# One written order of two thousand tokens in place of the priority scheduler, in an attention and MLP kernel on one core

## Chip, cores and metric

The kernel runs on one core of a Trainium2 chip. The metric is the device time of one execution in microseconds (us); less is better. The core's engines each work through their own queue in the order in which the program was laid out: TensorE (PE) multiplies, VectorE (DVE) and ScalarE (ACT) work elementwise, GpSimd (POOL) hardly takes part, and SyncE (SP) issues the DMAs. An instruction at the head of a queue that has to wait holds up all behind it.

## What is computed

Inputs of attention are q, k, v, a_re, a_im of shape (4, 8, 768, 48); the output of attention becomes 3072 tokens of 384, which go through an MLP with weights 384 x 2048 and 2048 x 384, all float32.

```
mag = np.sqrt(a_re * a_re + a_im * a_im)
scale = np.minimum(mag, 0.999) / (mag + 1e-06)
a_re_n, a_im_n = (a_re * scale, a_im * scale)
for t in range(S):                       # S = 768, per batch and head
    new_re = ar * S_re - ai * S_im       # ar, ai: a_re_n, a_im_n at t
    new_im = ar * S_im + ai * S_re
    S_re, S_im = (new_re + k[t] outer v[t], new_im)
    y[t] = q[t] @ S_re
h = x @ w_in                             # x: y as 3072 x 384
g = h - np.tanh(h)
out = g @ w_out
```

## The kernel before

The sequence is cut into six chunks of 128 positions. A *block* g (0 to 11) is one chunk of two batches: 256 tokens. A *unit* u (0 to 23) is one chunk of one batch; block g consists of the units 2g and 2g + 1. The names of the stages:

- *Gates* of a block: `gates_b` (magnitude: Ln and Exp on ACT), `gates_b2` (decay), `gates_c` (angle: Arctan, then running sums by matmuls with a triangle, line 220 or in f32 line 217), `gates_d` (cosine and sine) and `gates_e` (running sums, Exp into `g_e`, and the chunk's last row through a small DRAM buffer `hscr` into `hd`).
- `products` of a unit: q and k are multiplied by gates and waves on DVE, cast to an f16 pair (high part on ACT, remainder on DVE) and transposed, by DMA (`qT`, `kT`, line 408) or, for the first four units, which stay in f32, by TensorE. `vv` is the pair of v.
- `attention` of a unit (line 431): scores by matmul, masked on DVE into `af`, split into the pair `a`; the matmuls with the carried state `z` and with `vv` give y in PSUM; y is cast to f16 on ACT and its remainder taken on DVE (tile `x`), and one DMA transposes both into `xT`. Last comes the update of `z`.
- MLP of a block, in eight steps fp: `head` (line 510) is 18 matmuls of 256 columns into one of three PSUM buffers `h`, then tanh on ACT and h - tanh on DVE (tile `mt`); `split` makes the f16 pair `mg` of two steps; `tail` (line 540) is 12 matmuls of 384 columns into `o`. After step 7, o goes to the output by way of ACT and DMA.
- `decode`: 16 weight pairs come in as 64-bit words and are turned to f16 pairs, five operations on DVE and ACT each plus the remainder.

What sets the order: the text emits instructions by the lists START, FIRST, SECOND and CYCLE, which say after which head of a block which steps of other stages are issued, and each call carries a *kind* with an offset (OFFSET, for the first blocks EARLY), which the class `At` hands to `tc.high_priority`. The framework's priority scheduler then decides at build time the final order on each engine's queue and the buffers, from priorities and dependencies. Activations that need a table, and the table loads, are chained in the order of the text by `chained` (line 334). `tables` emits a load where the wanted set is not the current one. Most instructions are recorded at the wrapper's line 102, so groups are best told apart by their tiles.

Of the kernel before, what the change touches and what calls it, by code (L numbers as in the profile page):

```python
# [84 lines left out]

@with_exitstack
def tile_fast(ctx: ExitStack, tc: tile.TileContext, flag, a_in, qkv_in, win_in, wout_in, sq_c, vec_c, lim_c, out):
    nc = tc.nc
    V, G, A, T, SP = nc.vector, nc.gpsimd, nc.scalar, nc.tensor, nc.sync

    early = [True]

    class At:
        def __init__(self, eng, kind):
            self.eng, self.kind = eng, kind

        def __getattr__(self, n):
            f, offset = getattr(self.eng, n), (EARLY if early[0] else OFFSET)[self.kind]

            def call(*a, **k):  # L100
                with tc.high_priority(offset=offset):
                    return f(*a, **k)  # L102
# [23 lines left out]
    ps_a = ctx.enter_context(tc.tile_pool(name="ps_a", bufs=3, space=PSUM))  # L126

# [11 lines left out]
    araw = {}  # L139
    raws = {}  # L140

    def load_a(g):
        if g < NG:
            c, bp = divmod(g, 2)
            araw[g] = [sb.tile([P, 2 * HD], F32, name=f"a_raw{i}") for i in range(2)]
            for x in ((slice(0, HD), slice(HD, 2 * HD)) if g == 0 else (slice(0, 2 * HD),)):
                for t, i in zip(araw[g], range(2)):
                    SP("load").dma_start(out=t[:, x], in_=a_in[c * P:(c + 1) * P, bp, i, x])

    def load_qkv(u):  # L150
        if u < 2 * NG:
            c, b = divmod(u, B)
            raws[u] = sb.tile([P, 3, H, D], F32, name="qkv_raw", bufs=2)
            SP("load").dma_start(out=raws[u], in_=qkv_in[c * P:(c + 1) * P, b])

    load_a(0)
    vec = const.tile([P, 9], F32, name="vec")
    SP("load").dma_start(out=vec, in_=vec_c)
    sqc = const.tile([P, 4, P], F32, name="sqc")
# [98 lines left out]
    def gates_c(g, cols):  # L258
# [9 lines left out]
        for x in cols:  # L268
# [3 lines left out]
            if plain:  # L272
                continue
# [555 lines left out]
```

## Time and profile before

| what | us |
|---|---|
| three runs | 577.77, 577.37, 574.74 |
| median | 577.37 |
| profiled execution, span from first to last instruction | 570.2 |
| PE, DVE, ACT busy in it | 506.1, 452.8, 435.8 |
| first head of blocks 0, 1, 2, 3 begins | 69.8, 115.6, 158.0, 202.3 |
| first head of blocks 4 to 9 begins | 243.9, 285.4, 326.9, 368.4, 409.9, 451.1 |
| first head of blocks 10 and 11 begins | 489.4, 525.9 |
| last tail ends | 563.2 |

The profile gives the profiled execution's span and no device time beside it; the median of the runs is 7.2 us above that span. In the profile a group is written as line, engine, operation, out<-in; "idle before" is the time its engine stood still just ahead of its instructions and what ended most of that. PE's busy time is modelled at its ends. PEld are the weight loads, which run beside the matmuls. "L102" is the wrapper of `At`, so it tells nothing of the stage.

The first 70 us are spent on the gates, the weights and the f32 units of block 0, with TensorE mostly waiting. From there on blocks follow one another, every 41.5 us in the middle; while block g is projected, the attention of block g + 1 and the gates after it are worked in between. The last two blocks have less or no attention beside them.

### The profile page before, as it was taken

To read this page: it belongs to the slowest core of one execution; us is meant where nothing else is said; L and a number is where in the kernel's file an instruction comes from. 1 tells how busy PE (TensorE), PEld (TensorE's weight loads), DVE (VectorE), ACT (ScalarE), POOL (GpSimd) and SP (SyncE) were. 2 spreads that over 40 slices of the span, in tenths; PEclk is the share of its full clock that TensorE was granted. 3 is DMA by queue.
4 is the path that set the end of the run, shared out by engine and by line. 5 is a ranking of instruction groups with operands and counts; after the bars stand their busy time and mean duration, and the time that the engine had idled before them with its cause. 6 is when DMAs were issued, how large, how long until landed. Compare 5 with 4: busy or idle time off the path is not lost.

```text
span 570.2 us, 12229 instructions
## 1 busy us (share of the span) xinstructions
PE 506.1 (89%) x5058; PEld 389.4 (68%) x5058; DVE 452.8 (79%) x638; ACT 435.8 (76%) x784; POOL 2.3 (0%) x7
## 2 busy tenths in 40 slices
PE   2386399999999989989899899899899899999995
PEld 0164387876777767777677677687687677787772
DVE  4987999999898798798797897887986987953332
ACT  6978967998967967977968968959959959643442
POOL 1000000000000000000000000000000000000000
PEclk9976599999999999999999999999999999999998
DMA  7886822368184274286293383482672550730001
GB/s 253 244 313 179 256 63 51 76 135 188 24 199 130 49 165 133 44 142 160 57 190 100 79 168 99 101 165 81 126 150 71 130 144 15 130 90 15 29 1 33
DMA packets 133899, 68.08 MB, mean 119 GB/s; under 512 B 119982, under 2 KB 123694, under 8 KB 133836
## 3 DMA queue, kind: packets, MB, share of 16 engines
q1 hardware_dynamic: 133836, 67.23, 48.7%
q8 instruction: 41, 0.67, 0.5%
q14 instruction: 22, 0.18, 0.1%
HBM read 36.74 MB, written 4.78 MB: 73 GB/s over the span
## 4 chain that ended last, share of the span: by engine, by line
PE 44%; ACT 25%; DVE 16%; DMA 7%; issue 6%; SPq 1%; ACTq 0%; DVEq 0%
PE h L518 17%; PE o L549 15%; PE att L102 9%; DMA xT<-x 4%; ACT L102 4%; ACT a_raw L102 4%; ACT g_trig L102 3%; ACT mg L102 3%; ACT g_t L102 2%; DVE io L402 2%; DVE a_raw L102 2%; DVE qkv_raw L398 2%; DVE g_t L102 2%; PE att L217 2%; ACT mt L102 2%
## 5 line engine op out<-in xcount | busy, mean ns | idle before, releaser
L518 PE MATMUL h<-xT,w 128*128 128x256 f16 x1728 | 215.6, 274 | 23.1 <-DMA xT<-x 23.1
L549 PE MATMUL o<-w,mg 128*128 128x384 f16 x1152 | 206.1, 326 | 0.8 <-DVE mg L102 0.7
L518 PEld LDWEIGHTS <-w 128*128 128x128 f16 x1728 | 167.4, 98 | 54.6 <-DMA xT<-x 14.7
L549 PEld LDWEIGHTS <-mg 128*128 128x128 f16 x1152 | 110.6, 98 | 64.3 <-DVE mg L102 1.2
L102 DVE SCALAR_TENSOR_TENSOR mt<-h,mt 128x512 f32<-128x512 f32 x96 | 65.0, 686 | 40.0 <-ACT mt L102 39.5
L102 ACT ACTIVATE mt<-h 128x512 f32<-128x512 f32 x96 | 55.5, 590 | 43.4 <-PE h L518 43.2
L535 DVE SCALAR_TENSOR_TENSOR mg<-mt,mg 128x1024 f16<-128x1024 f32 x40 | 48.9, 1224 | 25.3 <-ACT mg L102 25.3
L102 ACT ACTIVATE mg<-mt 128x1024 f16<-128x1024 f32 x48 | 50.5, 1052 | 17.9 <-DVE mt L102 17.9
L102 ACT ACT_TABLE_LOAD x40 | 51.3, 1283 | 1.4 <-PEq L822 0.8
L102 PE MATMUL att<-qT,kT 96*128 96x128 f16 (+1 forms) x544 | 47.3, 235 | 1.1 <-ACT kT L102 0.7
L102 ACT ACTIVATE a_raw<-a_raw 128x768 f32<-128x768 f32 (+2 forms) x49 | 39.2, 802 | 1.7 <-DVE a_raw L102 1.7
L402 DVE TENSOR_TENSOR io<-qkv_raw,g_trig 128x768 f32<-128x768 f32 x40 | 36.9, 951 | 0.3
L119 DVE TENSOR_TENSOR qk<-io,qk 128x1536 f16<-128x1536 f32 x20 | 35.0, 1751 | 0.3 <-ACT qk L102 0.2
L102 DVE TENSOR_TENSOR a<-af,a 128x512 f16<-128x512 f32 x40 | 27.2, 684 | 8.5 <-ACT a L102 8.4
L102 ACT ACTIVATE a<-af 128x512 f16<-128x512 f32 x40 | 24.8, 626 | 11.8 <-DVE af L455 11.3
L102 PEld LDWEIGHTS <-kT 96*128 96x128 f16 x480 | 30.6, 97 | 3.2 <-DMA kT<-qk 0.8
L102 ACT ACTIVATE g_e<-att,vec 128x384 f32<-128x384 f32 x48 | 27.1, 572 | 4.4 <-PE att L217 4.3
L102 ACT ACTIVATE qk<-io 128x1536 f16<-128x1536 f32 x20 | 29.6, 1481 | 0.3 <-DVE io L402 0.3
L455 DVE TENSOR_TENSOR af<-att,sqc 128x512 f32<-128x512 f32 x36 | 24.5, 681 | 0.1
L102 DVE SCALAR_TENSOR_TENSOR g_t<-g_t,a_raw 128x768 f32<-128x768 f32 (+1 forms) x26 | 23.0, 889 | 0.7 <-ACT a_raw L102 0.7
L102 ACT ACTIVATE g_trig<-g_t 128x768 f32<-128x768 f32 (+1 forms) x26 | 20.3, 785 | 0.7 <-DVE g_t L102 0.6
L398 DVE SCALAR_TENSOR_TENSOR qkv_raw<-g_e,qkv_raw 128x768 f32<-128x768 f32 x20 | 19.0, 951 | 1.9 <-ACT g_e L102 1.9
(88 smaller groups left out, 602.4 us busy)
## 6 DMA issues: line engine op xcount, KB each, us to landing
qkv_raw<-in_qkv SPq DMA_DIRECT2D x24, 576.0 KB
a_raw<-in_a SPq DMA_DIRECT2D x22, 384.0 KB
io<-in_wout SPq DMA_DIRECT2D x16, 384.0 KB
io<-in_win SPq DMA_DIRECT2D x16, 384.0 KB
out_dram<-io SPq DMA_DIRECT2D x24, 192.0 KB
a_raw<-in_a SPq DMA_DIRECT2D x4, 192.0 KB
xT<-x SPq DMA_TRANSPOSE x24
hd<-hscr SPq DMA_DIRECT2D x20, 3.0 KB
```

The lines of the kernel that those rows point to most:

```text
L102: return f(*a, **k)
L119: by_name[ENGINE[which]](kind).tensor_tensor(**k)
L217: T("cum").matmul(c_ps[:, :HD], lhsT=tri32[which], rhs=hl[:, bb * HD:(bb + 1) * HD], start=True, stop=True)
L398: V("prod").scalar_tensor_tensor(out=x, in0=ee[:, :, sl], scalar=E_MAX, in1=x, op0=ALU.min, op1=ALU.mult)
L402: V("prod").tensor_tensor(out=f[:, i], in0=raw[:, i, :, None].broadcast_to([P, H, 2, D]), in1=tg[:, :, sl].rearrange("p r (h d) -> p h r d ...
L455: V("af").tensor_tensor(out=af.rearrange("p (j t) -> p j t", j=4), in0=s_ps.rearrange("p (j t) -> p j t", j=4), in1=(causal if plain else ...
L518: T("h").matmul(h_ps[:, j].rearrange("p (two t) -> p two t", two=2), lhsT=wi[ft][:, wp, kt * P:(kt + 1) * P], rhs=xT[:, :, xp, kt, :], sta ...
L535: V("glo").scalar_tensor_tensor(out=gg[:, 1], in0=th, scalar=2.0 ** SG, in1=gg[:, 0], op0=ALU.mult, op1=ALU.subtract)
L549: T("o").matmul(o_ps[:, tt, :DM], lhsT=gg[:, gp, fp % 2, j * 256 + tt * P:j * 256 + (tt + 1) * P], rhs=wo[ft][:, wp], start=(ft == 0 and n ...
```

## The change

All stages become generators ("streams"), named by a letter: T table load, c constants, A and Q loads, d decode (kind, pair), w, R and X statistics, B to E the gates of a block, p `products` of a unit, v its values, z the cast of the state, s scores (unit, half), y the matmuls to the transposed x, k the update of the state, h head, g split, o tail, O output. A stream yields after each instruction, or after each group of matmuls: h and o are yielded in two halves, 9 and 6 matmuls. `drive` walks through ORDER: each token advances its stream by one step, and `*n` by n steps; a T token always loads its table. The context `tc.manual_schedule()` makes the text's order the final one on all queues, and `At`, `copy`, `chained`, the lists and the offsets go. ORDER has 2,007 tokens, 2,089 steps. Tiles, buffer counts and the arithmetic stay; the constant 1.0 of the last check is set at the start. There are 52 T tokens. The diff, cut to its core (the passages of ORDER are from its start, the surroundings of block 0's first h, the passage around the start of block 6, and its end):

```diff
-LAG = 2
-START = (
-    "o3 i0 F0 F1 q0 i1 q1 p0 p1 B1 p0 i2 p1 o0 p0 b1 a0 p1 a1 a1 E1 C1 i7 a1 D1 a1 o6 a0 o4 i4 i5 o1 a0 o2 i3 B2 a0 "
-).split()
...
-CYCLE = tuple((int(i), x) for i, x in (y.split(":") for y in (
-    "0:p2 0:a1 3:p3 4:p2 4:p3 5:a2 5:a2 5:p3 5:a2 6:w0 6:a2 6:a2 6:a0 7:C2 7:a3 9:D2 10:B3 10:a3 10:E2 10:a3 11:a3 11:b3 11:p4 14:w1 "
-).split()))
...
+SETS = ("natural_log_exp_and_others", "trig_and_small", "sigmoid_and_others", "silu_and_others", "exp_and_others")
+ORDER = """
+A.0*2 T.0 B.0 A.0 c B.0*2 d.1.0 B.0 d.1.0 A.0 b.0*2 B.0 b.0*2 d.1.0 T.1 C.0 b.0 d.0.0 B.0 d.0.0 c E.0 b.0 d.1.1 d.1.0*2 C.0 d.1.0 Q.0 d.0.0 d.1.1 Q.1
+T.0 b.0 d.0.0 b.0 d.0.0 b.0 d.1.0 E.0 b.0 C.0 d.0.0 E.0 d.1.0 A.1 E.0 C.0 d.1.2 d.0.0 R.0 C.0 E.0 C.0 d.1.1 D.0 C.0 d.1.1 T.1 D.0 R.0 d.1.1 C.0 D.0*2
+d.1.2 v.1 R.1 C.0 D.0 p.0 A.1 d.0.0 D.0 d.1.1 d.0.3 p.0 T.0 E.0 p.0 p.1 R.1 p.0 B.1 p.0 p.1 d.0.3 p.0*2 B.1 p.1*3 d.0.4 v.0 p.1*2 d.1.2 d.0.2 p.0 p.1
+B.1 d.1.2 b.1 p.0*2 b.1 d.1.2 d.1.1 p.1 p.0*2 d.0.3 d.1.2 s.0.0 s.0.1 d.0.1 b.1 d.1.1 E.0 d.0.1 E.0 b.1 s.0.0 d.0.1 T.1 C.1 c b.1 p.1 Q.2 d.0.2 d.0.4
+p.1 d.0.1 C.1 d.0.3 C.1 s.0.1 d.0.1 d.0.5 d.0.3 d.0.1 C.1 d.1.2 d.0.5 C.1 d.0.3 d.0.1 C.1 d.0.3 d.1.2 C.1 d.0.1 p.1 Q.3 D.1 d.0.2 D.1 d.0.3 D.1 y.0
+d.0.2 d.0.6 d.0.5 R.2 y.0 d.0.4 d.0.5 s.1.0 d.0.2 s.1.1 d.0.5 d.0.4 C.1 A.2 s.1.0 v.2 y.0 A.2 d.0.4 y.0 d.0.2 y.0 T.0 B.2 E.1 B.2 s.1.1 d.0.4 y.1 B.2
...
+d.0.5*2 b.2 p.2*3 h.0.1 R.3 p.2 b.2 k.1 p.2 h.0.0 d.0.7 d.1.3 h.0.4 p.3 d.1.3 C.2 h.0.0 T.1 C.2 T.4 E.1 d.0.7 p.3 C.2 p.3 C.2 d.1.4 h.0.0 d.1.3 d.1.5
...
+k.12 s.13.1 E.6 o.4.7 O.4 y.12*2 B.8 O.4 s.13.1 k.13 O.4 p.14*2 v.15 h.5.5 g.5.1 s.13.0 o.5.0 h.5.6 h.5.4 b.8 s.13.1 b.8 O.4 p.15 y.12 p.14 b.8 o.5.0
+h.5.5 v.15 g.5.1 E.6 o.5.1 k.13 h.5.7 o.5.1 s.13.0 s.13.1 b.8 h.5.4 T.2 h.5.4 y.13 p.14 h.5.4 E.7 y.12 o.5.2 y.13 h.5.7 b.8 E.7 h.5.5 y.13 o.5.2 y.13
+y.12 s.14.1 v.14 h.5.7 h.5.5 b.8 s.14.0 v.14 y.13 g.5.2 b.8 s.14.1 o.5.3 C.8 h.6.0 E.8 y.13 p.15 C.8 o.5.3 g.5.2 C.8 T.4 E.8 C.8 Q.17 p.15 h.5.7 h.6.2
+s.14.0 h.6.0 o.5.4 C.8 h.6.3 p.15 o.5.4 h.6.2 z.14 s.14.0 E.8 Q.16 g.5.3 v.14 z.15 s.14.1 C.8 E.8 z.14 s.14.0 p.15 g.5.3 o.5.5 p.15 C.8*2 h.6.0*2 C.8
...
+h.11.7 o.11.3 g.11.2 o.11.4 g.11.2 o.11.4 h.11.7 o.11.5 g.11.3 o.11.5 g.11.3*2 R.23 o.11.6*2 o.11.7*2 X O.11 X*2 O.11*3
+"""
...
+def drive(streams, order):
+    live = {}
+    for token in order.split():
+        name, _, times = token.partition("*")
+        for _ in range(int(times or 1)):
+            if name not in live or name[0] == "T":
+                kind, *args = name.split(".")
+                live[name] = streams[kind](*map(int, args))
+            next(live[name], None)
+    for stream in live.values():
+        assert next(stream, "end") == "end"
+
...
-    early = [True]
-
-    class At:
-        def __init__(self, eng, kind):
-            self.eng, self.kind = eng, kind
-
-        def __getattr__(self, n):
-            f, offset = getattr(self.eng, n), (EARLY if early[0] else OFFSET)[self.kind]
-
-            def call(*a, **k):
-                with tc.high_priority(offset=offset):
-                    return f(*a, **k)
-            return call if offset else f
-
...
+    ctx.enter_context(tc.manual_schedule())
+
+    def cast(out, in_, scale=1.0):
+        A.activation(out=out, in_=in_, func=AF.Copy, scale=scale)
...
+    def tables(i):
+        table[0] = SETS[i]
+        A.preload_act_table_set(SETS[i])
+        yield
+
+    def act(func, **k):
+        assert table[0] in TABLES[func], (func, table)
+        A.activation(func=func, **k)
...
+    def mix(u):
+        g, bb = divmod(u, 2)
+        c = u // B
+        plain = u < PLAIN
+        qT = unit[u]["qT"]
+        y_ps = ps_a.tile([P, 512], F32, name="att")
+        if c > 0:
+            z16 = z16s[u]
+            for h in range(H):
...
+        cast(x16[:, 0], y_ps[:, :HD], ys)
+        yield
+        V.scalar_tensor_tensor(out=x16[:, 1], in0=y_ps[:, :HD], scalar=ys, in1=x16[:, 0], op0=ALU.mult, op1=ALU.subtract)
+        yield
+        if g not in xTs:
+            xTs[g] = sb.tile([P, 2, 2, KT, P], F16, name="xT", bufs=BUFS["xT"])
+        SP.dma_start_transpose(out=xTs[g][:, bb].rearrange("p two k t -> p (two k) t"), in_=x16.rearrange("p two e -> p (two e)"))
+        yield
+        A.activation(out=junk()[:, :HD // 8], in_=y_ps[:, :HD].rearrange("p (n s) -> p n s", s=8)[:, :, 0], func=AF.Square, scale=ys, accum_out=stat("x"))
...
+    drive({
+        "T": tables, "c": constants, "A": load_a, "Q": load_qkv, "d": decode, "w": weight_stats,
+        "B": ratio, "b": decay, "C": angles, "D": waves, "E": envelope,
+        "R": raw_stats, "p": keys, "v": values, "z": state, "s": scores, "y": mix, "k": update,
+        "h": head, "g": split, "o": tail, "O": emit, "X": check_stats,
+    }, ORDER)
```

More of the change, by code (lines that the diff above doesn't have):

```diff
@@ L137, in junk @@
         return sb.tile([P, 2, 512], F16, name="junk").rearrange("p a n -> p (a n)")
[L139 to L156, printed above, removed]
+    table = [None]
+    def tables(i):
[5 more added lines that the diff above has]
+        A.activation(func=func, **k)
     vec = const.tile([P, 9], F32, name="vec")
[L158 removed]
     sqc = const.tile([P, 4, P], F32, name="sqc")
[L160 removed]
     tri = const.tile([P, P], F16, name="tri")
[L162 removed]
     causal, mask, tri32, ident = sqc[:, 0], sqc[:, 1], (sqc[:, 0], sqc[:, 2]), sqc[:, 3]
@@ L277, in gates_c @@
+            if not plain:
+                ax = by_half(ai)
+                cast(hl[:, :, 0], ax, 1.0 / TWO_PI_F)
+                yield
+                V.scalar_tensor_tensor(out=hl[:, :, 1], in0=ax, scalar=1.0 / TWO_PI_F, in1=hl[:, :, 0], op0=ALU.mult, op1=ALU.subtract)
+                yield
         nf = sb.tile([P, W], F32, name="g_t1")
@@ new lines, in envelope, with raw_stats, keys @@
+                yield
+    unit = [{} for _ in range(2 * NG)]
+    def raw_stats(u):
+        sq = sb.tile([P, 3, D // 3], F32, name="rawsq")
+        A.activation(out=sq, in_=raws[u][:, :, u % H, :D // 3], func=AF.Square)
+        yield
+        V.tensor_reduce(out=stat("qkv", 3), in_=sq, axis=mybir.AxisListType.X, op=ALU.add)
+        yield
+    def keys(u):
+        g, bb = divmod(u, 2)
+        ee, raw = gate[g][0], raws[u]
+        sl = slice(bb * HD, (bb + 1) * HD)
+        wave = lambda: trig[g][:, :, sl].rearrange("p r (h d) -> p h r d", d=D)
+        if u < PLAIN:
@@ L412, in products, with values @@
+        yield
+        unit[u]["k"] = dst[:, 1]
+        for i in range(2):
+            dT = sb.tile([P, 2 * H, P], F16, name=("qT", "kT")[i], bufs=BUFS[("qT", "kT")[i]])
+            unit[u][("qT", "kT")[i]] = dT
+            SP.dma_start_transpose(out=dT, in_=dst[:, i].rearrange("p two h e -> p (two h e)"))
+            yield
+    def values(u):
+        v = raws[u][:, 2].rearrange("p h d -> p (h d)")
+        if u < PLAIN:
             vd = sb.tile([P, 512], F32, name="af", bufs=BUFS["af"])[:, :HD]
-            copy("vd", "vhi", vd, v, sVd)
@@ L465, in attention @@
-        a16 = [x[0] for x in a16]
-        y_ps = ps_a.tile([P, 512], F32, name="att")
-        if c > 0:
-            for h in range(H):
-                for n, (qp, zp) in enumerate(PASS):
-                    T("qu").matmul(y_ps[:, h * D:(h + 1) * D], lhsT=qT[0:K, qp * H + h], rhs=z16[0:K, zp, h * D:(h + 1) * D], start=(h == 0 and n == 0), stop=False)
-        yield "QU"
+        plain = u < PLAIN
+        kk, vv = unit[u]["k"], unit[u]["v"]
+        kv = ps_a.tile([P, 512], F32, name="att")
@@ L504, in attention @@
-        yield "Z"
+            for n, (kp, vp) in enumerate(PASS):
+                T.matmul(kv[:, h * D:(h + 1) * D], lhsT=kk[:, kp, h], rhs=vv[:, 2 + vp, h * D:(h + 1) * D], start=(h == 0 and n == 0), stop=(h == H - 1 and n == 2))
+        yield
+        z, src = z32[b][0:K], kv[0:K, :HD]
+        if c > 0:
+            V.scalar_tensor_tensor(out=z, in0=z, scalar=2.0 ** (SK + SV - SZ - STEP[-1]), in1=src, op0=ALU.mult, op1=ALU.add)
+            src = z
+            yield
+        hd = gate[g][1]
```

654 lines of the change are left out of this document (310 added, 344 removed).

## Prediction

> **What bounds the kernel now.** I read the page's busy line first, then the busy time of the engines in three stretches, then TensorE's waits.
>
> ```profile
> span 570.2 us, 12229 instructions
> PE 506.1 (89%) x5058; PEld 389.4 (68%) x5058; DVE 452.8 (79%) x638; ACT 435.8 (76%) x784; POOL 2.3 (0%) x7
> ```
>
> ```profile
> 0.00:69.80 69.80, 32.33 (x113) 23.79 (x114) 54.92 (x80) 56.03 (x99) 2.34 (x7) 0.79 0.79 248
> 69.80:158.00 88.20, 85.32 (x812) 67.61 (x812) 82.11 (x119) 78.34 (x136) 0.00 (x0) 0.98 0.40 92
> 158.00:570.20 412.20, 388.46 (x4136) 298.04 (x4133) 315.75 (x441) 301.43 (x551) 0.00 (x0) 0.99 0.46 103
> ```
>
> Columns of the second fence: stretch, length, then busy time of PE, PEld, DVE, ACT, POOL, granted clock, DMA share, GB/s. The stretches are cut at two first projections (h): block 0's starts at 69.76, block 2's at 158.01, and the rows of the timeline for these are
>
> ```profile
> 69.76 5.16 PE L518 MATMUL h<-xT,w 128*128 128x256 f16 x27 [9.19 <-DMA xT<-x]
> 158.01 2.13 PE L518 MATMUL h<-xT,w 128*128 128x256 f16 x18
> ```
>
> So there are three regimes. Until 69.8 TensorE has little to do and VectorE sets the pace (54.9 of 69.8). From there to 158.0 both are nearly full (PE 85.3, DVE 82.1 of 88.2), since the last weights are still decoded. From 158.0 on TensorE alone bounds: 388.5 of 412.2. Its idle time there is 23.7 us. Whom it waited for in that stretch, and the end of the chain of work that ended last:
>
> ```profile
> PE h L518 <- DMA xT<-x: 14.0, 7, 3.3
> PE att L220 <- ACT a_raw L102: 2.0, 8, 0.2
> PE o L549 <- DVE mg L102: 0.7, 1, 0.7
> ```
>
> ```profile
> 551.48 1.95 PE o L549 x12
> 553.43 1.97 PE h L518 x18
> 555.39 7.81 PE o L549 x48
> ```
>
> 14.0 us are seven waits for the transposed attention output xT at the head of a block, 2.7 are small waits, and 7.0 (570.2 - 563.2, where the last o ends) are the output's way home. 14.0 + 2.7 + 7.0 = 23.7, so the stretch is explained. In the two rows above it a full projection pair is 3.92 us without a gap, so PE's work itself is not compressible by an order. An order can only win in the 23.7 us and ahead of 158.0.
>
> The sums below are made against the span of the profiled execution, 570.2. The median of the three runs shown is 577.37, 7.2 more, and I add 7.2 to a span to get a time. A difference under 0.5% (2.9 us) is one that a measurement here can hardly tell from none.
>
> **Term 1, the start of block 2.** The new list puts 194 VectorE instructions ahead of block 2's first h; the old trace has 198 there (80 and 119 in the rows, one of them cut in two by the border). Sixteen weight pairs are decoded in both, and it is the same work but for four fewer on balance. What a short and a middling one cost:
>
> ```profile
> L102 DVE TENSOR_TENSOR a<-af,a 128x512 f16<-128x512 f32 x40 | 27.2, 684 | 8.5 <-ACT a L102 8.4
> L102 DVE TENSOR_SCALAR vv<-vv,vec 128x768 f16<-128x768 f16 x20 | 8.2, 411 | 0.0
> ```
>
> Four cost 1.6 to 2.7 us; I take 2.0 and get 54.9 + 82.1 - 2.0 = 135.0 us of VectorE work. The question is the idle time beside it: 14.9 us in the first stretch, 6.1 in the second. VectorE's waits in the first:
>
> ```profile
> DVE a_raw L102 <- ACT a_raw L102: 5.3, 2, 3.5
> DVE a L102 <- PE att L102: 2.6, 3, 1.0
> DVE x L102 <- ACT x L102: 2.0, 1, 2.0
> DVE w L102 <- ACT w L102: 1.3, 3, 0.9
> ```
>
> The first row is the very beginning (nothing is loaded yet), and the list begins the same way, so it stays. The other three the list fills: between the scores s.0.0 and the masking behind them stand two other VectorE instructions (the gate's lm, a decode's wlo), between y.0's cast and its remainder five (three of decodes, one mask, one value), and every wlo of a decode stands several places behind its whi. I count 2.6 + 2.0 + 1.3 = 5.9 us as gone, keep the rest: 9.0 + 6.1 = 15.1 idle. Start of block 2: 135.0 + 15.1 = 150.1. Bounds: 156.0 with the old 21.0 us of idle time, 144.0 if the 6.1 of the second stretch goes too. TensorE allows it: if block 0 begins 5.9 us earlier, at 63.9, and then needs 85.3 us less what is put off (next term), 82.4, plus its old 2.9 of idle time, it is there at 149.2.
>
> **Term 2, what is put off.** The list lets o trail h by more: ahead of block 2's first h it has 23 half tails of six matmuls, 138, where the old trace has
>
> ```profile
> L549 PE MATMUL o<-w,mg 128*128 128x384 f16 x156 | 28.3, 326 | 0.0
> ```
>
> by 158. Eighteen matmuls at 1.95/12 = 0.163 are 2.9 us that come later. The other TensorE work ahead of that point is the same.
>
> **Term 3, the block boundaries.** Old boundary, from the timeline (start, duration):
>
> ```profile
> 315.78 0.77 PE L477 MATMUL att<-vv,a 128*128 128x48 f16 x24
> 316.38 2.13 PE L518 MATMUL h<-xT,w 128*128 128x256 f16 x18
> 320.42 0.58 ACT L102 ACTIVATE x<-att,vec 128x384 f16<-128x384 f32 x1
> 321.50 0.61 DVE L102 SCALAR_TENSOR_TENSOR x<-att,vec,x 128x384 f16<-128x384 f32 x1
> 322.06 0.94 SPq L102 DMA_DIRECT2D hd<-hscr  x2
> 323.10 2.29 SPq L102 DMA_TRANSPOSE xT<-x  x1
> 326.91 1.26 PE L518 MATMUL h<-xT,w 128*128 128x256 f16 x10 [1.76 <-DMA xT<-x]
> ```
>
> The chain is: attention done (316.4), cast on ACT, remainder on DVE, transpose by DMA, first h at 326.9: 10.5 us, with 8.7 us of other matmuls as cover. 4.0 of the 10.5 the cast spent behind the gate's Exp calls on ACT; 1.0 the transpose spent behind the hd loads on SP's queue (x is done at 322.1, the issue is at 323.1). Without these two, 320.42 to 326.91 less 1.0 is 5.5 us.
>
> In the list I counted, for blocks 3 to 11, the matmuls between the second unit's y and the block's first h: half heads of 9 at 1.97/18, half tails of 6 at 1.95/12, gate sums as two matmuls of a tail's width, and the attention's small ones by
>
> ```profile
> 293.98 1.28 PE att L102 x36
> ```
>
> The cover is 6.7, 6.6, 8.7, 3.8, 10.4, 7.9, 4.7, 4.9, 6.9 us. ACT instructions between y and its cast: 0, 3, 2, 1, 8, 2, 1, 3, 0; DVE instructions between cast and remainder: 1, 3, 3, 0, 5, 0, 0, 0, 3. A block of the old trace gives their mean cost, 33.95/64 = 0.53 and 35.34/52 = 0.68:
>
> ```profile
> 285.40:326.90 41.50, 39.45 (x440) 30.47 (x440) 35.34 (x52) 33.95 (x64) 0.00 (x0) 1.00 0.54 119
> ```
>
> Chain less cover, where positive, with these queues in full: 2.5 (block 4), 2.2 (6), 2.7 (7), 1.3 (9), 2.2 (10), 0.6 (11): 11.5 us. With clear queues (5.5 everywhere): 1.7 + 0.8 + 0.6 = 3.1. With the old chain of 10.5 everywhere: 33.9. I take 8 for the old 14.0, nearer to the full queues, since two engines that are busy 82 and 85% of a block will mostly not have done those instructions before. On SP the list takes the hd loads away from just ahead of the transpose, but puts a transpose of k or the first unit's own there in some blocks; that is inside the bounds.
>
> **Term 4, twelve more table loads.** The list has 52 tokens T, the trace
>
> ```profile
> L102 ACT ACT_TABLE_LOAD x40 | 51.3, 1283 | 1.4 <-PEq L822 0.8
> ...
> 308.93 1.28 ACT L102 ACT_TABLE_LOAD   x1
> 310.22 0.84 ACT L102 ACTIVATE g_trig<-g_t 128x768 f32<-128x768 f32 x1
> ```
>
> so the instructions are not quite the same: 12 x 1.28 = 15.4 us more of ACT. Ahead of block 2 the list has 16, as the old trace has,
>
> ```profile
> L102 ACT ACT_TABLE_LOAD x16 | 20.5, 1283 | 1.0 <-PEq L822 0.8
> ```
>
> so the twelve fall into blocks 2 to 10, at 1.7 us a block, and ACT goes from 34.0 to 35.7 of 41.5. Queued behind a load are a tanh or a cast; three PSUM buffers of h and the put-off tails cover them. I cost it at nothing on the path; without cover it is 15.4. (The Trainium skill, "ScalarE: Activation LUTs", under "Table sets: the hidden batching unit", says to batch activation calls by table set; this speaks against the change. Its section "What ACT_TABLE_LOAD costs" gives 2.66 us a switch, load and drain, and by that the twelve would be an estimated 31.9. The trace disagrees on the drain: the next activation starts 0.01 us behind the load.)
>
> **Sum.** 150.1 + 388.5 + 2.9 + 2.7 + 7.0 + 8.0 = 559.2 us of span, against 158.0 + 388.5 + 2.7 + 7.0 + 14.0 = 570.2 before. Plus 7.2: **566.4**, 1.9% less.
>
> **Rivals.**
>
> *Nothing gained at either place.* VectorE's idle time ahead of block 2 remains 21.0, since in a fixed order another wait turns up for each that is filled (start 156.0), and the boundaries cost 14.0 as before: 156.0 + 388.5 + 2.9 + 2.7 + 7.0 + 14.0 = 571.1, time 578.3. For it: three engines above 80% in one fixed order, any duration that is judged wrong stalls all. Against: PE's waits outside xT are just 2.7 us in 412, so a fixed order does hold here.
>
> *xT late at every block: slower.* The cover is 6.7 us on average in the list, 8.7 in the old boundary. If the chain takes the old 10.5 us, because the cast still waits on ACT, which now has more to do, or because the transpose stands behind others on SP, the boundaries cost 33.9: 551.2 + 33.9 = 585.1, time 592.3. It decides for slower (above 580.3) when the waits exceed 21.9 us, a chain of about 9 us. For it: covers of 3.8, 4.7 and 4.9. Against: the Exp calls that made the 4.0 us are elsewhere in the list.
>
> *The loads on the path.* If the twelve loads delay what TensorE waits for, 559.2 + 15.4 = 574.6, time 581.8. Against it: ACT's 7.5 us of slack a block.
>
> *Both places better.* Start 144.0, boundaries 3.1: 548.2, time 555.4.
>
> **How the numbers follow.** The forecast has 0.45, "both better" 0.12, "nothing gained" 0.17, "xT late" 0.22, "loads on the path" 0.04. Faster by over 0.5% (below 574.5): 0.45 + 0.12 = 0.57. Within: 0.17. Slower: 0.22 + 0.04 = 0.26. The range leaves out the better half of "both better" and the upper half of "xT late": 554 to 590. The forecast's own case lies within 558 to 574.
>
> **What would show it.** Right: block 0's first h near 64 and block 2's near 150; VectorE's waits for the tiles a, x and w small ahead of it; seven to nine waits of PE for xT of about 1 us, 8 in all; 52 table loads and ACT at 451 us; first h to first h in the middle blocks near 40.5 instead of 41.5. Wrong: block 2's first h after 156, or PE's waits for xT above 19.0 us (the point at which 559.2 turns into 570.2), or a wait of PE for a tanh, a cast of the scores or a gate's value that the old list of waits does not have.

## The result, and the profile after

| | before | after | predicted |
|---|---|---|---|
| time, us (median of 4 runs each) | 576.71 | 541.83 | 566.4 (554 to 590) |
| lowest to highest | 574.74 to 577.77 | 541.15 to 542.72 | |
| span of the profiled execution | 570.2 | 539.4 | 559.2 |
| first h of block 0, of block 2 | 69.8, 158.0 | 60.0, 141.1 | 63.9, 150.1 |
| xT waits of TensorE behind block 2's first h | 14.0 | 0 | 8.0 |
| table loads | 40 | 52 | 52 |

The ratio is 0.9425, 95% interval 0.9379 to 0.9471: 34.9 us less, where 11.0 were forecast. The direction was right, the time lies outside the range. These are the opening lines of the profile after and its three stretches, cut as before at block 0's and block 2's first h (columns as in the prediction):

```profile
span 539.4 us, 12301 instructions
...
PE 503.4 (93%) x5058; PEld 390.5 (72%) x5058; DVE 448.3 (83%) x638; ACT 449.5 (83%) x796; POOL 2.9 (1%) x7
```

```profile
0.00:60.00 60.00, 36.01 (x137) 25.61 (x138) 50.33 (x77) 54.71 (x97) 2.91 (x7) 0.74 0.72 242
60.00:141.10 81.10, 79.15 (x772) 64.50 (x771) 80.94 (x114) 78.11 (x132) 0.00 (x0) 0.98 0.50 134
141.10:539.40 398.30, 388.28 (x4153) 300.38 (x4151) 316.98 (x449) 316.67 (x569) 0.00 (x0) 0.99 0.45 107
```

Read them against the old ones. Ahead of block 2, VectorE has 50.3 + 80.9 = 131.3 us of work in 141.1, so it stands idle for 9.9 us; it was 137.0 in 158.0, 21.0 idle. In the second stretch it has 0.2 us left of 81.1: it is the bound there. Behind block 2, TensorE's busy time is what it was (388.3 against 388.5), but it fills all of the stretch except for two small waits, and 9.1 us behind the last o, which ends at 530.3:

```profile
PE att L490 <- DMA kT<-qk: 0.4, 1, 0.4
PE att L550 <- DVE z L554: 0.4, 1, 0.4
```

No matmul waits for xT any more (a weight load waits 0.44 us for it at block 6 and 0.23 at block 7, beside matmuls that run). The boundary of block 6, from the timeline (start, duration), shows how it looks now:

```profile
294.37 0.77 PE L524 MATMUL att<-vv,a 128*128 128x48 f16 x24
...
295.44 0.58 ACT L172 ACTIVATE x<-att,vec 128x384 f16<-128x384 f32 x1 [0.85 <-DMA xT<-x]
...
296.05 0.62 DVE L530 SCALAR_TENSOR_TENSOR x<-att,vec,x 128x384 f16<-128x384 f32 x1
...
296.70 1.21 SPq L534 DMA_TRANSPOSE xT<-x  x1
...
299.47 0.39 PE L572 MATMUL h<-xT,w 128*128 128x256 f16 x2
```

Attention ends at 295.14, the first h starts at 299.47: 4.3 us, where the same two points of the old boundary are 10.4 apart (316.55, the end of the row at 315.78, and 326.91). Nothing stands between the four steps: the cast starts 0.3 us behind the matmuls, the transpose 0.03 us behind the remainder, and its issue takes 1.21 us instead of 2.29. In blocks 3 to 11 the way takes 4.3 to 10.3 us, and each time there was that much other work for TensorE.

The table loads are these:

```profile
L189 ACT ACT_TABLE_LOAD x52 | 66.7, 1283 | 1.6 <-PEq L833 0.8
```

### The profile page after: what moved, and what is told of

Its sections match the earlier page's. It is cut to its first block, busy times and chain, and to the rows that moved or that the text cites. A ratio compares the mean times of both kernels' runs of the same rounds, so it can differ in the third digit from the quotient of the medians.

```text
span 539.4 us, 12301 instructions
## 1 busy us (share of the span) xinstructions
PE 503.4 (93%) x5058; PEld 390.5 (72%) x5058; DVE 448.3 (83%) x638; ACT 449.5 (83%) x796; POOL 2.9 (1%) x7
## 4 chain that ended last, share of the span: by engine, by line
PE 67%; DVE 14%; ACT 8%; DMA 5%; issue 3%; SPq 1%; ACTq 0%; DVEq 0%
PE o L604 29%; PE h L572 27%; PE att L490 4%; DMA kT<-qk 2%; PE att L524 2%; PE att L515 2%; PE att L280 2%; PE att L550 1%; ACT L189 1%; DVE w L255 1%; DVE wtmp L250 1%; DVE mt L581 1%; ACT a_raw L194 1%; DMA io<-in_win 1%; DVE wtmp L248 1%
## 5 line engine op out<-in xcount | busy, mean ns | idle before, releaser
L604 PE MATMUL o<-w,mg 128*128 128x384 f16 x1152 | 215.9, 326 | 0.3 <-DVE w L255 0.3
L572 PE MATMUL h<-xT,w 128*128 128x256 f16 x1728 | 212.7, 273 | 0.9 <-DVE mt L581 0.8
L604 PEld LDWEIGHTS <-mg 128*128 128x128 f16 x1152 | 109.2, 98 | 57.6 <-issue 0.7
L590 DVE SCALAR_TENSOR_TENSOR mg<-mt,mg 128x1024 f16<-128x1024 f32 x48 | 58.4, 1218 | 13.5 <-ACT mg L172 13.5
L172 ACT ACTIVATE mg<-mt 128x1024 f16<-128x1024 f32 x48 | 50.3, 1052 | 9.2 <-DVE mt L581 4.8
L493 DVE TENSOR_TENSOR af<-att,sqc 128x512 f32<-128x512 f32 x40 | 27.3, 683 | 9.7 <-PE att L490 9.6
L490 PE MATMUL att<-qT,kT 96*128 96x128 f16 x480 | 33.1, 219 | 0.6 <-DMA kT<-qk 0.4
L611 ACT ACTIVATE io<-o 128x384 f32<-128x384 f32 x24 | 11.5, 483 | 11.7 <-PE o L604 11.5
L172 ACT ACTIVATE x<-att,vec 128x384 f16<-128x384 f32 x24 | 13.7, 570 | 8.9 <-DMA xT<-x 5.0
L194 ACT ACTIVATE a_raw<-a_raw 128x768 f32<-128x768 f32 (+1 forms) x26 | 20.6, 794 | 0.3
L530 DVE SCALAR_TENSOR_TENSOR x<-att,vec,x 128x384 f16<-128x384 f32 x24 | 14.7, 611 | 5.9 <-ACT x L172 5.9
```

The costliest lines, as they stand in the source:

```text
L172: A.activation(out=out, in_=in_, func=AF.Copy, scale=scale)
L194: A.activation(func=func, **k)
L490: T.matmul(s_ps[:, j * P:(j + 1) * P], lhsT=kT[0:K, kp * H + h], rhs=qT[0:K, qp * H + h], start=(j == 0 and n == 0), stop=(j == 3 and n == 2))
L493: V.tensor_tensor(out=af.rearrange("p (j t) -> p j t", j=4), in0=s_ps.rearrange("p (j t) -> p j t", j=4), in1=(causal if plain else mask)[ ...
L572: T.matmul(h_ps[:, j].rearrange("p (two t) -> p two t", two=2), lhsT=weight[0][2 * fp + j][:, wp, kt * P:(kt + 1) * P], rhs=xT[:, :, xp, k ...
L590: V.scalar_tensor_tensor(out=gg[:, 1], in0=th, scalar=2.0 ** SG, in1=gg[:, 0], op0=ALU.mult, op1=ALU.subtract)
```

## Experiments

Where two lists are joined or the old order is edited, the list has one token for each instruction. The calls of those kernels are held back until their token comes, so that any order on the queues can be written. Most of their instructions are recorded under one helper line, and their rows are read by tile. The kernel before was timed again beside each group of runs, with medians from 574.25 to 576.86; gains below are against the one of the same group. The new kernel has its 541.83 from the first group alone, so what is said against it crosses groups whose old medians differ by up to 2.6 us.

### Is it the order, and in which half does the gain lie?

**The old order as a list.**

```diff
-ORDER = the new list
+ORDER = the old order, read off the old program, 6474 tokens
```

> The old order written out as a list, one token for each instruction, and emitted as the new kernel emits its own. Theory (the order is all that counts, not who emits it): the old time, 575 to 579 us. Rival (part of the gain comes from emitting by hand instead of by the scheduler): clearly less, 545 to 570 us.

Measured: 575.07 us (before 576.2), ratio 0.9994, 0.9956 to 1.0033. So it makes no difference who emits the instructions; the order counts. The run tells a second thing. It has the old order on every queue, yet its profile is not the one on which I built: block 2 starts at 154.1 instead of 158.0, and these are blocks 3, 4 and 6 (the columns of the stretches; the last three are the granted clock, the DMA share and GB/s):

```profile
198.75:243.22 44.47, 42.21 (x441) 31.71 (x441) 34.23 (x49) 32.66 (x60) 0.00 (x0) 0.94 0.50 108
243.22:284.79 41.57, 39.45 (x441) 30.48 (x441) 35.41 (x51) 33.83 (x64) 0.00 (x0) 1.00 0.55 117
326.73:370.19 43.46, 41.13 (x441) 31.28 (x441) 35.49 (x51) 33.96 (x64) 0.00 (x0) 0.96 0.53 116
```

The same 441 matmuls cost 39.45 us of TensorE at a clock of 1.00, 41.13 at 0.96 and 42.21 at 0.94. All three blocks begin with a wait for xT, of 3.42, 2.00 and 2.23 us. So such a wait can be followed by a slower block. In the profile that I read all of blocks 3 to 9 stood at 1.00: behind block 2 it was a lucky execution. Ahead of block 2 it was an unlucky one: this run and the six others below that keep the old start have block 2 at 154.1 to 156.0, not at 158.0.

**New start, old rest, and the other way round.**

```diff
-ORDER = the new list
+ORDER = the new list up to block 2's first h, then what is left, in the old order
```

> The new list up to block 2's first h, then the old order for what is left. Theory (start and boundaries are two gains that add up): first h of block 2 near 141, xT waits of TensorE back at 14 us, small waits back at 2.7; time 541.8 + 14.0 + 1.9 - 2.1 = 555.6 us, 552 to 560. Rival (the early start is borrowed, what was put off comes back as waits later): 565 to 577 us.

```diff
-ORDER = the new list
+ORDER = the old order up to block 2's first h, then what is left, in the new list's order
```

> The old order up to block 2's first h, then the new list for what is left. Theory (two gains that add up): first h of block 2 near 158, xT waits of TensorE near 0; time 541.8 + 16.9 = 558.7, less up to 2.9 us of tails already done: 555 to 560 us. Rival (the boundaries are only covered because the new start leaves more tails over): xT waits of 5 to 14 us and 564 to 573 us.

Measured: 568.36 us for the new start (7.8 less than before; ratio 0.9892, 0.9832 to 0.9952), 554.9 for the new rest (21.3 less; 0.9643, 0.96 to 0.9686). The second agrees with the theory but for 0.1 us of its range: no xT wait, block 2 at 154.4, where 158 was expected. It also means that the start is worth 554.9 - 541.8 = 13.1 us with the new rest behind it. The first missed, the rival's range holds it. Block 2's first h came at 145.9, not at 141: all that the new list puts off beyond that point was laid ahead of it by the join. I moved the join.

```diff
-ORDER = the new list
+ORDER = the new list up to block 3's first h, then what is left, in the old order
```

> The new list up to block 3's first h, then the old order for what is left. Theory (the new start's gain is real; with the border at block 2 it was lost because the work that the list puts off was all laid ahead of block 2's first h): block 3's first h near 178 where the old order has 199 to 202, then six old boundaries with some 11 us of xT waits: 576 - 21 = 555, range 552 to 560 us. Rival (put-off work costs the same wherever it comes): 563 to 569 us.

Measured: 557.39 us, 16.9 less (0.9711, 0.9657 to 0.9765), as the theory said, though block 3's first h came at 186.6 and not at 178: part of the put-off work was again laid ahead of the join. xT waits were 11.9 us in six boundaries. This 16.9 holds the boundary of block 3 as well, 3.3 us of xT wait in the old profile; without it 13.6 are left for the start. The start is thus worth some 13 us by either join, what lies behind it 21, and they add up to the 34.4 to 34.9.

### What made the old transposes late?

Three edits of the old order, at the boundaries of blocks 3 to 9 (block 6's tokens as the example).

```diff
 y.13            # remainder of x
-Q.16 E.7*2      # bulk qkv load, two hd loads
 y.13            # transpose
+Q.16 E.7*2
```

> The old order, only SP's queue changed: at the boundaries of blocks 3 to 9 the two hd loads and the bulk qkv load go behind the second unit's transpose instead of ahead of it. Theory (the transposes are late and long because of the loads ahead): issue right when x is done, 1.2 us instead of 2.3 to 2.9, so first h 2.1 us or more earlier; waits of 1.5 to 2.2 us go, block 3's 3.3 falls to about 1; xT waits 1 to 2 us in all and no drops of the granted clock behind them: 576.2 - 13 - 4 = 559, range 557 to 563 us. Rival (the transposes' own time is what it is, only the 1.0 us in the queue goes): 7 us of xT waits left, 567 to 570 us.

```diff
+y.13            # cast of x, ScalarE; then its remainder, VectorE
 E.7*4           # the four Exp, and what hangs on them
-y.13
```

> The old order, only ScalarE's and VectorE's queues changed: at the boundaries of blocks 3 to 9 the cast of x and its remainder go ahead of the four Exp of the gate's envelope and of what hangs on them; SP's order stays, so the transpose stays behind the hd loads, and these wait for the Exp. Theory (SP's queue holds the transpose back, whatever ScalarE does): x is done 3 us earlier, the transpose is not issued earlier; xT waits 13 to 20 us, 574 to 582 us. Rival (the 4.0 us of the cast behind the Exp are the cause): waits near 0, 556 to 562 us.

Both edits together:

> Both changes to the old order: cast of x ahead of the Exp, and the loads behind the transpose. Theory (the boundary's chain is these two queues): chain of 5 us or less under 8.7 us of cover, no xT wait at blocks 3 to 9: 576.2 - 14 - 4.5 = 557.7, range 555 to 561 us, the same as the old start with the new rest (554.9) but for 2 to 3 us. Rival (the new list wins something else behind block 2): 562 us or more.

Measured: loads behind 558.04 us (16.5 less than before; 0.9705, 0.9647 to 0.9763), as the theory said; cast first 583.48 (8.9 more; 1.0133, 1.0067 to 1.02), 1.5 above the theory's range and far from the rival's; both 561.26 (13.3 less; 0.9744, 0.9688 to 0.98), between theory and rival. ScalarE's queue, in which I had put 4.0 us, is worth nothing: with the loads behind, the cast still starts 3.9 us behind attention's end and the first h comes 8.43 to 8.48 us behind it, without a wait of a matmul, because that is just the old cover. With both edits the cast starts 0.9 us behind, and the first h still comes after 8.3 to 8.4 us. With the cast first alone it is slower. First SP's queue at the old boundary of block 6, with the bulk load at 321.61 ahead of the hd loads, then the same in the run with the cast first:

```profile
321.61 0.36 SPq L102 DMA_DIRECT2D qkv_raw<-in_qkv  x1
322.06 0.94 SPq L102 DMA_DIRECT2D hd<-hscr  x2
323.10 2.29 SPq L102 DMA_TRANSPOSE xT<-x  x1
```

```profile
323.75 0.24 SPq L273 DMA_DIRECT2D hscr<-g_e  x1
326.16 0.36 SPq L273 DMA_DIRECT2D qkv_raw<-in_qkv  x1
326.61 0.94 SPq L273 DMA_DIRECT2D hd<-hscr  x2
327.61 2.36 SPq L273 DMA_TRANSPOSE xT<-x  x1
```

In the second x was done at 323.41, 4.2 us ahead of its transpose. The bulk load at the head of the queue could not be issued before VectorE had read the old contents of its buffer. The edit had pushed that product back, it ended at 326.13, and all behind the load stood still until then. Moving both cost 3 us against moving the loads alone, with other waits (3.5 us for the output's copy, 4.4 for the angle's pair).

Which load is it? Only the hd loads behind, then only the bulk load behind:

```diff
-Q.16 E.7*2
+Q.16
 y.13            # transpose
+E.7*2
```

> The old order with only the two hd loads moved behind the second unit's transpose at blocks 3 to 8; the bulk qkv load stays ahead. Theory (hd holds the queue for 1.0 us and makes the issue 2.3 instead of 1.2 us, and the bulk load delays the landing by 1.5): 2.1 of the 3.6 us gained, xT waits of about 1 us at block 3, 0 to 0.5 at the others, 1.5 at block 9: 3 us in all; 560 to 564 us. Rival (the bulk load alone is the cause): 570 to 577 us.

```diff
-Q.16 E.7*2
+E.7*2
 y.13            # transpose
+Q.16
```

> The old order with only the bulk qkv load moved behind the second unit's transpose at blocks 3 to 9; the two hd loads stay ahead. Theory (either load ahead is enough for the wait, and their delays do not add: hd costs 1.0 us in the queue and makes the issue 2.3 instead of 1.2 us, the bulk load costs 2.2 us on the way; with both behind there was next to nothing to spare): xT waits of about 2 us at blocks 3 to 8, none at block 9, 9 to 13 in all, 567 to 573 us. Rival (the bulk load alone is the cause): waits near 0, 557 to 560 us.

Measured: hd alone 574.24 us (before 574.25; ratio 0.9998, 0.9962 to 1.0034), the bulk load alone 557.56 (19.3 less; 0.9684, 0.9647 to 0.9722). Both expectations favoured the wrong side: it is the bulk load. SP's queue in the two runs, hd behind first:

```profile
322.10 0.36 SPq L275 DMA_DIRECT2D qkv_raw<-in_qkv  x1
322.62 1.22 SPq L275 DMA_TRANSPOSE xT<-x  x1
```

```profile
310.99 0.89 SPq L275 DMA_DIRECT2D hd<-hscr  x2
312.66 1.22 SPq L275 DMA_TRANSPOSE xT<-x  x1
313.93 0.57 SPq L275 DMA_DIRECT2D qkv_raw<-in_qkv  x1
```

In the first the transpose is issued 0.03 us behind x, and xT waits are still 13.5 us, since it is long on its way:

```profile
PE h L275 <- DMA xT<-x: 13.5, 7, 2.2
```

In the chain of work that ended last, each DMA stands with its time from issue to landing. Hd-behind kernel, then the new kernel:

```profile
322.62 4.98 DMA xT<-x
```

```profile
292.62 2.74 DMA xT<-x
296.70 2.73 DMA xT<-x
```

With 576 KB issued 0.5 us ahead of it the transpose takes 4.98 us, without it 2.73. Why the hd loads make no difference shows when the landing is counted from the bulk load's issue. In five traces with that load ahead (the kernel before, the old list, cast first, hd behind, and the new kernel with loads ahead, below) the transposes in this chain at blocks 4 to 9 land 4.7 to 5.7 us behind the issue of the bulk load, whether they are issued 0.4 or 2.3 us behind it. What stands between the two costs nothing there. Only at block 3 it does: 6.8 to 6.9 us with hd between, 5.4 without, and a wait of 1.9 us instead of 3.3. In the second run the hd loads were issued at 311, 1.7 us before the transpose, so they held nothing up: in the old order they had stood behind the bulk load, which waited for its buffer. (The Trainium skill, "DMA: Bandwidth & Descriptors", section "Queues, rings and completion order", says that on each DMA engine the descriptors of a queue are taken in the order of its ring. The trace agrees, with 2.2 us more behind a bulk load.)

**The reverse, in the new kernel.**

```diff
+Q.17            # bulk load; likewise Q.12, Q.20, Q.22
 y.13            # transpose
 ...
-Q.17
```

> The new kernel with one bulk qkv load (576 KB) moved to just ahead of the second unit's transpose, at blocks 4, 6, 8 and 9, where the list has it behind. Theory (a bulk load ahead makes the transpose land later, by 0.4 us in the queue and some 1.5 us on its way, the list's time to spare there is 0.2, 0, 1.8 and 0.7): xT waits of 1.7, 1.9, 0.1 and 1.2, 5 us in all: 545 to 549 us. Rival (only the small hd loads, of which this moves none, matter): 0 to 1.5 us, 541 to 543 us.

Measured: 551.32 us, 9.5 more than the new kernel (ratio to before 0.9605, 0.9562 to 0.9647). The sign is right, the size about double. Block 6:

```profile
298.59 0.36 SPq L233 DMA_DIRECT2D qkv_raw<-in_qkv  x1
299.00 1.22 SPq L534 DMA_TRANSPOSE xT<-x  x1
```

x was done at 297.44; the load waited for its buffer until 298.59 (v's remainder, the last to read it, ended at 298.56), which I had not counted, and the transpose landed 4.54 us behind its issue. Waits of 3.4 and 4.0 us at blocks 6 and 9 (none at 4 and 8), and behind both of them the clock fell (0.93 and 0.95).

**The old rest with the loads behind, after the new start.** The join at block 3 from above, and the first edit of this section at blocks 4 to 9.

> The new list up to block 3's first h, then the old order with the hd and bulk loads moved behind the second unit's transpose at blocks 4 to 9. Theory (behind the start the new list wins by the freed transpose and by nothing else of weight): the 11.9 us of xT waits and 1.7 of dropped clock go: 557.4 - 13.6 = 543.8, range 541 to 546 us. Rival (the new list's other moves, covers, tails put off, casts, are worth something too): 548 to 552 us.

Measured: 547.11 us (0.9491, 0.9457 to 0.9525), between the two: 5.3 us above the new kernel. No xT wait is left; TensorE waits 5.7 us: for the angle's pair (2.4 and 0.2), the output's copy (2.0) and the MLP's pair mg (1.1), where the new kernel has the 0.8 shown above. So the new rest also removes small waits: 5 us with the new start, and without it some 3 (554.9 against 557.6 and 558.0), which is no more than the groups differ by.

### Do table loads cost nothing?

**Every load twice.**

```diff
-T.4
+T.4*2           # each of the 36 T tokens behind block 2's first h
```

> The new kernel with each of the 36 table loads behind block 2's first h issued twice: 36 x 1.28 = 46.2 us more of ScalarE, 317 to 363 us of the 398 us there. Theory (loads are covered while ScalarE has slack): under 6 us more, 542 to 548 us. Rival (loads lie on the path): all 46 us, 588 us; half of them, 565 us.

Measured: 542.6 us. This tells nothing of loads: the trace has 52, because a load that directly follows another one is merged with it when the program is built. It is a second measurement of the new kernel, 0.8 us from the first. The same again with an instruction in between, all 36 and then 12:

```diff
 T.4 h.4.5
+T.4             # 36 times; then behind every third T only
```

> The new kernel with 36 more table loads that stay: behind block 2's first h each load is issued once more, behind the next ScalarE instruction, so that the built program has 88 (loads that follow each other directly had been merged into one). 36 x 1.28 = 46.2 us more of ScalarE, 317 to 363 of the 398 us there. Theory (a load is covered unless it stands ahead of the cast of x at a boundary): 0 to 6 us more, 542 to 548 us. Rival (loads lie on the path): 46 us more, 588 us; half of them, 565 us.

> The new kernel with 12 more table loads behind block 2's first h, one behind every third, each behind the ScalarE instruction that follows: the dose of the change itself, 15.4 us of ScalarE. Theory now (in a fixed order ScalarE's idle time is not where an unplanned load falls, as with the 36, which cost 0.98 us each): 9 to 12 us more, 551 to 554 us. Rival (the prediction's: covered by 7.5 us of slack a block, at this dose): 0 to 2 us, 541 to 544 us.

Measured: the theory missed at 36 loads, and its successor held at 12. With 36 more 577.45 us, 35.6 more than the new kernel (ratio to before 1.0054, 1.0024 to 1.0084); with 12 more 551.65, 9.8 more (0.957, 0.9541 to 0.96). That is 0.99 and 0.82 us for each load of 1.28. TensorE's two largest entries of waits, with 36 and with 12:

```profile
PE o L606 <- ACT io L613: 10.2, 7, 2.7
PE h L574 <- DVE mt L583: 7.5, 7, 1.8
```

```profile
PE o L605 <- ACT io L612: 2.7, 3, 1.2
PE h L573 <- DVE mt L582: 1.5, 4, 0.7
```

They are those for the output's copy out of the single PSUM buffer of o, and for the three buffers of h. ScalarE had 317 of 398 us of work, so it was idle a fifth of the time, and still most of each load reached the end. (Taken by the ratios to the old kernel of the same group, a load costs 1.01 and 0.70 us.)

**Loads ahead of the cast.**

```diff
+T.2*3           # the current table; blocks 3 to 11
 y.13            # cast
```

> The new kernel with three more loads of the current table right ahead of the cast of x in the second unit of blocks 3 to 11: 27 loads, 34.6 us of ScalarE, fewer than the 36 loads of the run before that cost under 1 us. Theory (the list's cover at each boundary holds with 0 to 2.2 us to spare, 6.3 in all by the time from the end of the transpose's issue to the first h, of which 1.56 is the least): each boundary pays 3.85 less its spare time and less ScalarE's idle time there, together 20 to 28 us of xT waits, and drops of the clock behind them: 562 to 580 us. Rival (ScalarE's slack takes it as it took the 36): under 548 us.

Measured: 548.13 us, 6.3 more (0.9526, 0.9472 to 0.9579), far below the theory and 0.1 above the rival. Neither was put to the test, for of three loads in a row one was left: 9 loads, 11.5 us, and 0.70 us for each (0.65 by the ratios). By the spare time of each boundary, as in the expectation, 1.28 at a time would come to 6.7 us. The waits named are just in part those for xT (2.2 us), so the agreement of the sums proves little.

### What is the filling at the start worth?

```diff
 d.1.0           # high part of a weight pair, ScalarE
+d.1.0           # remainder, VectorE
 ...
-d.1.0
```

> The new kernel with its fillings undone ahead of block 2's first h: 31 VectorE instructions (the remainder of 15 weight pairs, 12 maskings, 4 remainders of x) stand directly behind the instruction of ScalarE or TensorE that they wait for. Theory (the start gained because other VectorE work fills these waits): VectorE's idle time ahead of block 2 rises from 9.9 by 6 to 14 us, block 2's first h to 147 to 155, 547 to 556 us. Rival (the gain is work put off and a better order of loads): under 545 us.

Measured: 563.53 us, 21.7 more than the new kernel (ratio to before 0.9784, 0.9746 to 0.9822). Its two stretches ahead of block 2, and what VectorE waited for there:

```profile
0.00:68.40 68.40, 32.96 (x137) 23.61 (x138) 50.78 (x77) 55.38 (x97) 2.58 (x7) 0.73 0.65 213
68.40:162.80 94.40, 83.96 (x771) 67.27 (x770) 81.69 (x113) 78.03 (x131) 0.00 (x0) 0.94 0.42 115
```

```profile
DVE w L255 <- ACT w L172: 12.4, 9, 2.5
DVE a_raw L293 <- ACT a_raw L194: 5.1, 2, 4.5
DVE x L530 <- ACT x L172: 4.3, 3, 3.0
```

VectorE's work is what it was (132.5 against 131.3), its idle time is 162.8 - 132.5 = 30.3 instead of 9.9, and block 2 begins 21.8 us later, at 162.8. The whole difference of the time is made there. The filling carries the new start; its size was set too low, probably since one late remainder delays the weights, the heads and the instructions queued behind. The run undoes more than the old order did (30.3 us idle, where the old list has 17.1), so it doesn't say what part of the 13 us the filling is. The first join says something of that: with the put-off work laid back, block 2 began at 145.9 with 135.9 us of VectorE work and 10.1 idle, against 154.1 with 137.0 and 17.1 in the old list. Of the 13 us some 7 are idle time that is gone, some 6 work moved behind.

## Why the prediction was wrong in size

The forecast sum and the measured one, term by term; the two columns add up to 566.4 and, but for 0.1 of rounding, to 541.8.

| term | predicted | measured | difference |
|---|---|---|---|
| start of block 2 | 150.1 | 141.1 | -9.0 |
| TensorE's work behind it, put-off tails included | 391.4 | 388.3 | -3.1 |
| small waits | 2.7 | 0.8 | -1.9 |
| way home | 7.0 | 9.1 | +2.1 |
| boundaries | 8.0 | 0 | -8.0 |
| from span to median | 7.2 | 2.4 | -4.8 |

**Term 1, the start (9.0 us).** The mechanism was right: undoing the fillings gives up more than the whole gain of the start. The step that failed is "keep the rest: 9.0 + 6.1". I had listed VectorE's waits of the first stretch alone and kept the second's idle time as it was, but it was the same kind of idle time. Here are the old kernel's waits for these tiles up to block 2, which I should have asked for, and then the largest of the new kernel's:

```profile
DVE x L102 <- ACT x L102: 2.7, 2, 2.0
DVE a L102 <- PE att L102: 2.6, 3, 1.0
DVE mg L102 <- ACT mg L102: 2.3, 1, 2.3
DVE w L102 <- ACT w L102: 1.5, 4, 0.9
```

```profile
DVE a_raw L293 <- ACT a_raw L194: 4.9, 2, 4.5
DVE g_t L308 <- ACT a_raw L194: 2.9, 3, 1.8
DVE wtmp L250 <- ACT io L172: 0.9, 1, 0.9
```

The waits for x, a, mg and w are gone, but for 0.4 us, and what is left is the beginning with the first gate. Of the 16.9 us by which block 2 starts earlier, 11.1 are idle time (I had 5.9) and 5.7 are VectorE work (I had 2.0). The work is put off, not saved: laid back ahead of block 2 by the first join it put the start at 145.9. My bound of 144.0 was not low enough, since it took the work as fixed. The work put off costs nothing later: behind block 2 TensorE's waits are 0.8 us in all.

Not all of the 16.9 is the change. The execution that I read began block 2 late: in the old list's trace, with the same order and the same 137.0 us of VectorE work, it is at 154.1, and the waits for a, x and w in its first stretch, which I had counted as 5.9 us, are 1.8, 0.5 and 0.7. Against the 154.1 to 156.0 of the seven runs with the old start the new start gains 13 to 15 us. That so much of a sum from one profile is one execution's chance I did not allow for.

**Term 2, the put-off tails (3.1 us with TensorE's work).** The tails were put off as counted: 1015 rows of o are recorded behind block 2's first h where 998 were. Yet TensorE's busy time did not rise by their 2.9 us. The start-to-start spacing of neighbouring matmuls is the same in both traces, 0.109 us for h and 0.163 for o, so no matmul became faster. The old 388.5 thus held about 3 us that were not matmul work. A row's mean (273 ns for h) is longer than the spacing, so each stop shows the end of a matmul as busy time, and the new order stops less; whether that is all of it was not tried.

**Term 3, the boundaries (8.0 us).** The step that failed is "I take 8 for the old 14.0, nearer to the full queues". I charged the chain's two delays to ScalarE's queue (4.0) and to the hd loads (1.0) and called 5.5 the clear chain. By the runs, 4.0 us of ScalarE's queue lay inside the cover and hd cost nothing beyond block 3; what made the waits was the bulk load ahead of the transpose, 2.2 us on its way and more when the load had to wait for its buffer. Its row in the old boundary, at 321.61, just ahead of hd, is not among those that I quoted; the first h follows 5.3 us behind it. My 5.5 took the landing from a block in which it was delayed; undelayed the chain is 4.3, and the list's covers (3.8 to 10.4 by my count, 4.3 to 10.3 in the trace) hold it everywhere, at block 6 without anything to spare. That the Exp calls were elsewhere in the list was true and did not matter.

**From span to time (4.8 us).** "I add 7.2 to a span to get a time" was the hidden failure. Each run lists both, and time less span is 1.7 to 1.9 us in both kernels: by that the old profiled execution took an estimated 572.0. The other 5.4 us were the distance of a lucky execution from the median. Three blocks at a lower clock cost 6.1 us in the old order's own second run (42.21, 41.13 and 40.96 where 39.45, 39.45 and 39.29 are usual), and the profile that I read had none. They come behind xT waits. With the waits they go too, and with them much of the spread: over all groups the old kernel's times lie between 570.1 and 579.8, the eight of the new one, its second measurement included, between 541.2 and 544.8. So a boundary cost more than its wait; the bulk load's 14 us of waits were worth 16.5 to 19.3.

**Term 4, the twelve loads.** The outcome was right, the reason was not. TensorE waits for nothing of ScalarE's behind block 2's first h, so the 12 cost nothing there. But "ACT's 7.5 us of slack a block" does not cover a load: 12 loads that the list didn't plan for cost 9.8 of their 15.4 us. That the list's own loads are free because the order around them was made with them in it is a guess. (The Trainium skill, "ScalarE: Activation LUTs", under "Table sets: the hidden batching unit", says to batch activation calls by set. The runs agree that a load is not free in a busy kernel, at 0.70 to 0.99 us each. The 2.66 us a switch of its section "What ACT_TABLE_LOAD costs" does not show in the old trace: the load of 1.28 us at 308.93 begins 0.02 us behind one activation and ends 0.01 us ahead of the next.) What the change's own 12 would save if they could be left out was not tried.

**Small waits and way home.** The small waits fell from 2.7 to 0.8. The way home grew by 2.1 us, though its instructions are the same; the same list's end took 7.2 us in the run with the old start. I have no cause for it.

**Rivals.** "Both places better", at 0.12, was the case that came; its 144.0, 3.1 and 7.2 were all too high. "xT late at every block", at 0.22, rested on ScalarE's queue, which the runs cleared, or on the transpose standing behind others on SP. The second is real, though not in this list: four bulk loads put ahead cost 9.5 us.

## What to carry to other kernels

Look at the DMA queue before the engines' queues when a small transfer is late: a bulk load just ahead of it delays it twice, by the wait for its own buffer at the head of the queue and by its bytes on the way, and moving that one load behind in the old order gained 19.3 us, where the whole change gained 34.9. Price a stop of TensorE at more than its length, and do not carry the distance from one profiled execution to the median over to the new kernel: it may be made of what the change removes. Where a sum rests on waits, read them in more than one execution. An engine's idle share was no cover for added work in these fixed orders; ask of each added instruction what is queued behind it, and who waits for that.

## What the runs showed of the hardware

In seven executions with old boundaries or with loads laid ahead of the transpose, I set the wait at each block's first h beside that block's granted clock and busy time. Behind 17 waits of 1.48 to 1.86 us the clock was 1.00 every time. Behind 20 waits of 1.92 to 2.69 us it fell to 0.96 in ten, with 41.1 us of TensorE work instead of 39.45 in a middle block. Behind 6 waits of 3.34 to 3.97 us it fell to between 0.93 and 0.96 in five. Cut into slices of 1 us, a block at 0.96 has the clock at 0.50 for 3.4 us in its first 4, and at 1.00 from then on (old list, block 6; cast first, block 5; hd behind, block 3). Behind the waits of 3.4 us at the old list's block 3 and the load-ahead run's block 6 the clock is 0.50 for 5.7 and 5.9 us. (The Trainium skill, "TensorE: Matmul & The Clock Gate", section "What's actually happening", has the clock halved after an idle window of about 3.4 us that runs freely. The trace agrees on the half and, in the blocks at 0.96, on the length of 3.4 us; but waits of 1.9 us were already enough in some cases, shorter than the window.)

The same 1.28 us table load cost between 0.70 and 0.99 us of the kernel's time, with ScalarE idle a fifth of it.
